# Four wide blocks in place of three, an attention plan that keeps SBUF work out of GpSimd's spans, and query loads into three buffers

## The chip, the cores and the metric

The kernel runs on one core of a Trainium2 chip. The metric is the device time of one execution in microseconds. The core has TensorE (PE; PEld are its weight loads), VectorE (DVE), ScalarE (ACT), GpSimd (POOL) and SyncE (SP), whose queue issues all DMAs here.

## The reference

Two parts, in float32:

```
proj = einsum('bhsd,df->bhsf', x, w_phi)          # x is q or k: 8 x 8 x 576 x 64, f = 128
proj = proj - max(abs(proj), axis=-1)
phi  = concat([exp(proj), exp(-proj)], axis=-1)   # 256 features
kv = einsum('bhsf,bhsd->bhfd', phi(k), v);  z = sum(phi(k), axis=2)
attn = einsum('bhsf,bhfd->bhsd', phi(q), kv) / (einsum('bhsf,bhf->bhs', phi(q), z) + 1e-6)
x = attn, tokens by heads*dims: 4608 x 512
out = gelu(x @ w_in) @ w_out                      # 512 -> 2048 -> 512, gelu with erf
```

## The kernel before, in words

The work is planned as a list of operations on engines (`plan.op`), each with an assumed cost, a rank, the buffers it uses, and for PE a kind. `Plan.order` goes through a schedule: it takes the engine whose next operation can start first, and on it, of those that could start within 0.02 us, the one of lowest rank. An operation can start when what it reads is done and its buffers' slots are free. The result is one fixed order per engine, which the chip runs with semaphores; the assumed costs are not used on the chip. Two things in that planner matter here. For an operation of VectorE that reads no PSUM (`psum=False`) and overlaps a GpSimd operation, it adds a cost `BLOCKED` of 0.9 us once per GpSimd operation. And PE changes between feed-forward work (`kind` "f") and attention work in lumps (`LUMP`, `LINGER`).

**Attention** goes by batch b = 0 to 7, in two halves g of four heads. `k_quad` loads keys (kt) and values (vt), projects them (pk), takes the maximum (mx) and the difference on VectorE, the exponentials (ek) on ScalarE, and sums into kv. `q_pair` handles two heads and half the tokens: a load qt, the projection pq, a copy pc on ScalarE, `partition_all_reduce` with absmax on GpSimd (mb), a difference on VectorE, two exponentials (ef), the numerator pn, and a store to x_d. For b = 0 and 1 (`EB`, `ND`) the denominator comes out of the matmul too; from b = 2 on VectorE forms un and GpSimd sums it over partitions (db). `quotients` loads the denominators (dc), inverts them and stores r_d.

**Weights**: 16 pieces w_i and 16 pieces w_o arrive as 64-bit numbers (raw); `split_weight` turns each into two float32r parts with two steps on ScalarE and five on VectorE. w_o15 is the last.

**Feed-forward**: `block` (narrow, 256 tokens) loads xr and rb, makes xh and xl, and runs 192 matmuls of 256 columns (ph) and 96 of 512 columns (po). `wide_block` (512 tokens) uses seven products in place of eight for the first layer: 336 matmuls of 256 columns (pa, pb) and 192 of 512 (po_po, po_pp), against 384 and 192 in two narrow blocks. It needs combinations of the weights, which `combos` forms on VectorE (tiles sw and sh) and stores in s_d, from where each wide block loads them (s). `JW` is the number of pairs of narrow blocks: with 6 there are 12 narrow and 3 wide blocks. Operations of combos and wide blocks are planned after the last 60 operations of attention (`GATE`). A block's output passes through ob (two slots) to a store.

Of the kernel before, what the change touches and what calls it, by code (L numbers as in the profile page):

```python
# [10 lines left out]
F32 = mybir.dt.float32  # L11
F32R = mybir.dt.float32r
# [15 lines left out]
P = 128  # L28
HS = S // 2
# [30 lines left out]
class Plan:  # L60
# [57 lines left out]
    def order(self, bias):  # L118
        free = dict(self.slots)
        slot_free_at = {t: [0.0] * n for t, n in self.slots.items()}  # L120
        turn = dict.fromkeys(self.slots, 0)
        engines = {}
        for o in self.ops:
            engines.setdefault(o.eng, [])
        clock = dict.fromkeys(engines, 0.0)
        table = [None]
        cand = {e: [] for e in engines}
        for o in self.ops:
            if o.wait == 0:
                cand[o.eng].append(o)  # L130
        done = []
        n = len(self.ops)

        gelus, left_at, dma, dge = [0], [0.0], [0.0], [0.9]

        def start_of(o):
            t = max(clock[o.eng], o.ready)
            if o.table == "exp" and table[0] == "gelu" and gelus[0] % (2 * STICK):
                t = max(t, left_at[0] + PATIENCE)
            seen = {}  # L140
            for b in o.bufs:
                if not b.held and b.tag is not None:
                    f, i = slot_free_at[b.tag], seen.get(b.tag, 0)
                    if len(b.line) <= i or b.line[i] is not b:
                        return None
                    when = f[(turn[b.tag] + i) % len(f)]
                    if when is None:
                        return None
                    t = max(t, when)
                    seen[b.tag] = i + 1  # L150
            return t


        clk = {"i": 0, "full": False, "busy": 0.0}
        last, first = ["f"], {}
        taken = []

        def run(t, work, duty):
            while work > 1e-9:
                i = int(t / self.WINDOW + 1e-9)  # L160
                while clk["i"] < i:
                    use = clk["busy"] / self.WINDOW
                    clk["full"] = use > (0.5 if clk["full"] else self.BUSY)
                    clk["i"] += 1
                    clk["busy"] = 0.0
                speed = 1.0 if clk["full"] else 0.51
                dt = min((i + 1) * self.WINDOW - t, work / speed)
                clk["busy"] += dt * duty
                work -= dt * speed
                t += dt  # L170
            return t

        while len(done) < n:
            best = None
            for e, lst in cand.items():
                if not lst:
                    continue
                opts = []
                for o in lst:
                    t = start_of(o)  # L180
                    if t is not None:
                        opts.append((t, o))
                if not opts:
                    continue
                t0 = min(t for t, _ in opts)
                lim = max(t0, clock[e]) + 0.02
                hold = 0.0
                if e == "pe" and last[0] == "f":
                    t_of = {id(o): max(o.ready, first.setdefault(o.n, t)) for t, o in opts}
                    there = [o for t, o in opts if t <= lim and o.kind != "f"]  # L190
                    if sum(o.cost for o in there) < LUMP and all(lim - t_of[id(o)] < LINGER for o in there):
                        hold = 4000.0
                key = None
                for t, o in opts:
                    if t <= lim:
                        k = o.rank
                        if e == "act" and o.table is not None and o.table != table[0]:
                            k += bias
                        if o.kind != "f":
                            k += hold  # L200
                        if key is None or (k, o.n) < key[0]:
                            key = ((k, o.n), t, o)
                if best is None or key[1] < best[1]:
                    best = key
            if best is None:
                raise RuntimeError("no operation can go")
            _, t, o = best
            cand[o.eng].remove(o)
            cost = o.cost
            if o.eng == "act" and o.table is not None and o.table != table[0]:  # L210
                cost += self.SWITCH
                table[0] = o.table
            if o.eng == "pe":
                if self.SHAPE[last[0]] != self.SHAPE[o.kind]:
                    cost += self.BEHIND[last[0]] + self.BEFORE[o.kind]
                last[0] = o.kind
            if o.eng == "dve" and not o.psum:
                for span in taken[-4:]:
                    if t < span[1] - 0.3 and t + cost > span[0] + 0.3 and not span[2]:
                        span[2] = True  # L220
                        cost += BLOCKED
            if o.eng == "pool":
                taken.append([t, t + cost, False])
            o.start, o.end = t, run(t, cost, o.duty) if o.eng == "pe" else t + cost
            if o.nbytes:
                dge[0] = max(dge[0], t) + 0.55
                dma[0] = max(dma[0], dge[0] + 0.75) + o.nbytes / 350.0
                o.late = dma[0] + 0.15 - o.end
            if o.table == "gelu":
                gelus[0] += 1  # L230
                left_at[0] = o.end
            clock[o.eng] = o.end
            for b in o.bufs:
                if b.tag is not None and not b.held:
                    f = slot_free_at[b.tag]
                    b.slot = turn[b.tag]
                    f[b.slot] = None
                    turn[b.tag] = (b.slot + 1) % len(f)
                    b.held = True
                    assert b.line.pop(0) is b  # L240
                b.left -= 1
                if b.left == 0 and b.tag is not None:
                    slot_free_at[b.tag][b.slot] = o.end + o.late + self.HOP[o.eng]
            for u in o.users:
                u.wait -= 1
                u.ready = max(u.ready, o.end + o.late + (self.HOP if u.eng != o.eng else self.SAME)[o.eng] + (MARGIN if u.eng == "pe" != o.eng and o.end > 130.0 else 0.0))
                if u.wait == 0:
                    cand[u.eng].append(u)
            done.append(o)
        self.done = done  # L250
        return max(o.end + o.late for o in done)
# [37 lines left out]
def fused_kernel(ctx: ExitStack, tc: tile.TileContext, qT, kT, va, w_st, w_in, w_out, out):  # L289
    nc = tc.nc  # L290
# [11 lines left out]
    sb = {t: plan.pool(spool, t, n) for t, n in SLOTS.items()}  # L302
    PS = dict(pp=1, kv=1, pn=1, ph=2, po=1)
    ps = {t: plan.pool(ppool, t, n, False) for t, n in PS.items()}
    op = plan.op
# [167 lines left out]
    def q_pair(b, p, kvs, rank, halves=(0, 1)):  # L473
# [4 lines left out]
        for half in halves:  # L478
            nm = f"{b}_{p}_{half}"
            ss = slice(half * HS, half * HS + HS)  # L480
            qt = sb["qt"]([P, HS] if b < EB else [P, 2, HS], F32, f"qt_{nm}")
            if b < EB:
                op("sp", 0.06, lambda qt=qt, ss=ss: nc.sync.dma_start(out=qt(), in_=qT[b, p, :, ss]), w=[qt], kb=147, **k(1))
            else:
                for i in range(2):
                    op("sp", 0.06, lambda qt=qt, ss=ss, i=i: nc.sync.dma_start(
                        out=qt()[64 * i : 64 * i + 64], in_=qT[b, p, :, ss].rearrange("(j d) t -> d j t", j=2)), w=[qt], kb=147, **k(1))
# [172 lines left out]
    def combos(rank):  # L660
        plan.stream = "c"
        lo, hi = slice(0, 256), slice(256, 512)
        for q in range(4):
            for i in range(2):
                k = dict(rank=rank((2 * q + i) / 8))
                ws = [sb["ob"]([P, 512], F32, f"sw_{q}_{i}_{x}") for x in range(2)]
                hs = [sb[tag]([P, 512], F32R, f"sh_{q}_{i}_{tag}") for tag in ("db", "qt")]
                for x in range(2):
                    c = wi[i + 2 * x, q]
                    tt("dve", dve(512), ws[x], lambda c=c: c()[:, 0].bitcast(F32), lambda c=c: c()[:, 1].bitcast(F32), ALU.add, [c], [ws[x]], also=[*ws, *hs], **k)  # L670
# [17 lines left out]
    def wide_block(j, rank):  # L688
# [55 lines left out]
        for u in range(NU):  # L744
# [3 lines left out]
            sm = {}  # L748
            for s in (2, 3, 1, 4):
                m = sm[s] = sb[RING[s - 1]]([P, 2, 2, P], F32R, f"s{s}_{j}_{u}")  # L750
                op("sp", 0.06, lambda m=m, q=q, e=e, s=s: nc.sync.dma_start(out=m().bitcast(F32), in_=s_d[q]()[SUMS.index(s), e]), r=[s_d[q]], w=[m], kb=262, rank=rk - 20)
            A = ps["ph"]([P, 2, TB], F32, f"pa_{j}_{u}")
            Bk = ps[("kv", "pn")[u % 2]]([P, 2, TB], F32, f"pb_{j}_{u}")
            own = lambda c, f, q=q: (lambda i, w: wi[c + i, q]()[:, w, f % 4 * P : f % 4 * P + P], [wi[c, q], wi[c + 1, q]])
# [98 lines left out]


SB = 2
JW = 6
AHEAD = 1.5
AHEADW = 1.5
MARGIN = 0.8
CR = 100.0  # L860
CSPAN = 100.0
GATE = 60
T15 = 901.4
BIAS = 40
STICK = 2
PATIENCE = 2.5
URGE = -1000.0
EARLY = 37.5
WPACE = 3.996
WSPAN = 24.5  # L870
WARM = 4
EARLY_PK = ("pp", "po")
EARLY_E = ("ek", "xh", "ek", "xl")
BLOCKED = 0.9
HOLD2 = 0.0
EB = 2
KB = 0
EPACE = 20.0
TF = 90.0
ND = 2  # L880
LUMP = 2.5
LINGER = 3.0
PAIR_K = 0.43
PAIR_Q = 0.7
PAIR_N = 1.18
PAIR_V = 0.125
PULL = -2000.0
LEAD = 167.4
HOLD = 44.6
WR = -13.5  # L890
ATR = -21.1
T0 = 57.4
VERBOSE = False


# [36 lines left out]
```

## Time and profile before

| | |
|---|---|
| median of 3 runs | 1150.15 us (1148.31 to 1151.35) |
| the profiled execution | 1147.43 us, of which the span in the profile is 1145.7 us |
| PE busy | 1097.1 us, 96% of the span |
| DVE, ACT, POOL busy | 696.2, 662.2, 321.5 us |
| mean granted clock of TensorE | 0.98 |

The shares are means over stages. Up to about 207 us the weights are converted and attention of the first batches runs; up to about 790 us attention and narrow blocks are interleaved; then there are narrow blocks alone, and from about 875 us the three wide blocks.

### The profile page before, as it was taken

The numbers are of one execution on the slowest core, as the hardware profiler recorded it, in microseconds if no ns is written. First come the engines' busy times: TensorE is split into PE (matmuls) and PEld (weight loads), VectorE is DVE, ScalarE is ACT, GpSimd is POOL, SyncE is SP. The second block draws the span as 40 slices with busy tenths as digits, with TensorE's granted clock in tenths as the row PEclk, the third lists the DMA queues.
The fourth block names the chain that finished last, engine by engine and source line by source line (L and its number), as shares of the span: only waits on it lengthen the run. The fifth ranks groups of instructions, "written<-read, shape, count | busy, mean of one in ns | idle before, by whom it ended". The sixth has DMA issues, their size and how long they took to land.

```text
span 1145.7 us, 22254 instructions
## 1 busy us (share of the span) xinstructions
PE 1097.1 (96%) x8952; PEld 920.4 (80%) x8952; DVE 696.2 (61%) x1153; ACT 662.2 (58%) x1045; POOL 321.5 (28%) x116
## 2 busy tenths in 40 slices
PE   7878987999999999999999999999999999999997
PEld 4545766888887888888888888889889888898986
DVE  6897889665856867656466566554655534534331
ACT  5776857767777787776878778762112222222322
POOL 3323023343644546352445445450000000000000
PEclk9998987999999999999999999999999999999999
DMA  7676631324141332413132231205543624623420
GB/s 248 222 230 215 198 104 33 95 64 129 48 124 43 93 83 86 106 62 102 55 93 80 79 88 49 69 18 125 152 129 115 190 84 115 196 94 114 136 83 37
DMA packets 112439, 125.59 MB, mean 110 GB/s; under 512 B 27648, under 2 KB 87200, under 8 KB 112336
## 3 DMA queue, kind: packets, MB, share of 16 engines
q1 hardware_dynamic: 112336, 124.17, 36.6%
q8 instruction: 70, 1.15, 0.4%
q14 instruction: 33, 0.27, 0.1%
HBM read 96.57 MB, written 27.56 MB: 108 GB/s over the span
## 4 chain that ended last, share of the span: by engine, by line
PE 72%; DVE 9%; DMA 6%; issue 4%; SPq 3%; ACT 3%; POOL 2%; DVEq 0%; ACTq 0%; POOLq 0%
PE po L308 18%; PE ph L308 18%; PE kv L308 6%; PE pb L308 5%; PE po_pp L308 5%; PE pn L308 5%; PE po_po L308 5%; PE pa L308 4%; PE pq L308 3%; PE pk L308 3%; POOL mb L513 1%; SPq L708 1%; DMA qt<-in_qT_dram 1%; DMA rp<-r_d 1%; DVE gl L334 1%
## 5 line engine op out<-in xcount | busy, mean ns | idle before, releaser
L308 PE MATMUL ph<-xh,w_i 128*128 128x256 f32 x1536 | 299.9, 284 | 1.6 <-DVE gl L334 1.2
L308 PEld LDWEIGHTS ph<-xh,w_i 128*128 128x128 f32 x1536 | 248.2, 190 | 9.6 <-issue 2.2
L308 PE MATMUL po<-w_o,gh 128*128 128x512 f32 x768 | 246.4, 402 | 1.9 <-ACT ob L328 1.9
L513 POOL PARTITION_ALL_REDUCE mb<-pc x64 | 147.8, 2311 | 285.6 <-ACT pc L328 247.1
L548 POOL PARTITION_ALL_REDUCE db<-un x48 | 175.3, 3652 | 161.6 <-DVE un L545 123.4
L308 PE MATMUL ph<-xl,w_i 128*128 128x256 f32 x768 | 218.7, 285 | 0.0
L308 PEld LDWEIGHTS po<-w_o,gh 128*128 128x128 f32 x768 | 137.7, 190 | 31.4 <-issue 2.2
L308 PE MATMUL po<-w_o,gl 128*128 128x512 f32 x384 | 152.9, 398 | 0.6 <-DVE gl L334 0.6
L308 PEld LDWEIGHTS ph<-xl,w_i 128*128 128x128 f32 x768 | 146.1, 190 | 3.3
L519 ACT ACTIVATE ef<-pc 128x576 f32<-128x576 f32 x128 | 83.1, 680 | 59.1 <-DVE pc L334 58.8
L334 DVE TENSOR_TENSOR gl<-ph,gh 128x512 fp32r<-128x512 f32 x96 | 65.8, 686 | 84.5 <-ACT ph L636 81.2
L308 PEld LDWEIGHTS kv<-vt,ek 128*64 128x64 f32 (+1 forms) x2560 | 85.6, 140 | 36.7 <-ACT ek L447 14.1
L635 ACT ACTIVATE gh<-ph 128x512 fp32r<-128x512 f32 x96 | 57.5, 599 | 90.5 <-PE ph L308 83.1
L308 PE MATMUL kv<-vt,ek 128*64 128x65 f32 (+1 forms) x2560 | 97.7, 228 | 9.6 <-ACT ek L447 9.3
L308 PE MATMUL pn<-ef,kvn 128*64 128x288 f32 (+1 forms) x512 | 98.1, 425 | 1.2 <-ACT xo L328 1.0
L635 ACT ACT_TABLE_LOAD x76 | 97.5, 1283 | 1.5 <-PE ph L308 0.3
L308 PEld LDWEIGHTS po<-w_o,gl 128*128 128x128 f32 x384 | 73.0, 190 | 18.5 <-DVE gl L334 1.6
L794 ACT ACTIVATE gh<-pa 128x512 fp32r<-128x512 f32 x24 | 14.4, 599 | 123.1 <-PE po_pp L308 86.1
L447 ACT ACTIVATE ek<-ek 128x512 f32<-128x512 f32 (+1 forms) x120 | 70.1, 587 | 24.8 <-DVE ek L334 23.0
L334 DVE TENSOR_TENSOR pc<-pc,mb 128x576 f32<-128x576 f32 x64 | 65.4, 1021 | 29.7 <-POOL mb L513 29.4
L430 DVE TENSOR_REDUCE mx<-pk 128x4 f32<-128x512 f32 (+1 forms) x80 | 50.5, 631 | 50.2 <-PE pk L308 50.0
L308 PEld LDWEIGHTS pn<-ef,kvn 128*64 128x64 f32 (+1 forms) x512 | 39.6, 139 | 32.5 <-issue 7.5
(90 smaller groups left out, 1699.5 us busy)
## 6 DMA issues: line engine op xcount, KB each, us to landing
s<-s_d SPq DMA_DIRECT2D x96, 256.0 KB
qt<-in_qT_dram SPq DMA_DIRECT2D x112, 144.0 KB
vt<-in_va_dram SPq DMA_DIRECT2D x16, 585.0 KB
kt<-in_kT_dram SPq DMA_DIRECT2D x16, 576.0 KB
out_dram<-ob SPq DMA_DIRECT2D x36, 256.0 KB
raw_i<-in_w_in_dram SPq DMA_DIRECT2D x16, 512.0 KB
raw_o<-in_w_out_dram SPq DMA_DIRECT2D x16, 512.0 KB
x_d<-xo SPq DMA_DIRECT2D x48, 144.0 KB
```

The costliest lines, as they stand in the source:

```text
L308: return tc.keep_in_program_order(nc.tensor.matmul(*a, **kw))
L334: op(eng, cost, lambda: e.tensor_tensor(out=dst(), in0=a(), in1=b(), op=o), r=r, w=w, **kw)
L430: op("dve", dve(256 * n, True), lambda xs=xs, mx=mx: nc.vector.tensor_reduce(out=mx()[:, 0].rearrange("p (j i) -> p j i", j=2), in_=xs(), ...
L447: op("act", act(256 * n, b < SB), lambda at=at, es=es, s=s: nc.scalar.activation(es[s](), at(), AF.Exp, scale=1.0 - 2.0 * s), r=[of], w=[e ...
L513: op("pool", 2.2, lambda mb=mb, pc=pc: nc.gpsimd.partition_all_reduce(mb(), pc(), P, bass_isa.ReduceOp.absmax), r=[pc], w=[mb], **k(1))
L519: op("act", act(2 * HS), lambda ef=ef, pc=pc, s=s: nc.scalar.activation(ef()[:, s], pc(), AF.Exp, scale=1.0 - 2.0 * s), r=[pc], w=[ef], ta ...
L548: op("pool", 3.7, lambda db=db, un=un: nc.gpsimd.partition_all_reduce(db(), un(), P, bass_isa.ReduceOp.add), r=[un], w=[db], **k())
L635: op("act", act(2 * TB, True) + 0.016, lambda gh=gh, ph=ph: nc.scalar.activation(gh(), ph(), AF.Gelu), r=[ph], w=[gh], table="gelu", rank= ...
L708: op("sp", 0.06, lambda b=b, i=i, h=h, s=s, n=n, o=o, z=z, to=rp[z]: nc.sync.dma_start(out=to()[64 * i : 64 * i + 64, :, o : o + n], in_=r ...
L794: op("act", act(2 * TB, psum) + 0.016, lambda gh=gh, at=at: nc.scalar.activation(gh(), at(), AF.Gelu), r=[at], w=[gh], table="gelu", rank= ...
```

## The change

`JW` becomes 5: 10 narrow and 4 wide blocks. The planner no longer adds a cost for VectorE operations without PSUM in a GpSimd operation; it moves their start to the end of a span that begins with the GpSimd operation and lasts 1.4 us for the maximum (`LOCK_MAX`) and 2.4 us for the sum (`LOCK_SUM`). Operations that read PSUM may start inside. In the batches 0 and 1 the query loads use three tags (qt, gh, gl) in turn. `combos` takes its tiles from ek, mb and pc in place of ob, db and qt, and a wide block's loads of s are planned after all stores to s_d. Ranks and paces are new numbers.

```diff
+            if o.eng == "dve" and not o.psum and taken and taken[-1][0] <= t < taken[-1][1]:
+                t = taken[-1][1]
             return t
...
-            if o.eng == "dve" and not o.psum:
-                for span in taken[-4:]:
-                    if t < span[1] - 0.3 and t + cost > span[0] + 0.3 and not span[2]:
-                        span[2] = True
-                        cost += BLOCKED
             if o.eng == "pool":
-                taken.append([t, t + cost, False])
+                taken.append((t, t + (LOCK_MAX if cost < 3.0 else LOCK_SUM)))
...
-            qt = sb["qt"]([P, HS] if b < EB else [P, 2, HS], F32, f"qt_{nm}")
+            qt = sb[("qt", "gh", "gl")[(2 * p + half) % 3] if b < EB else "qt"]([P, HS] if b < EB else [P, 2, HS], F32, f"qt_{nm}")
...
-                ws = [sb["ob"]([P, 512], F32, f"sw_{q}_{i}_{x}") for x in range(2)]
-                hs = [sb[tag]([P, 512], F32R, f"sh_{q}_{i}_{tag}") for tag in ("db", "qt")]
+                tags = ("ek", "ek") if i == 0 else ("mb", "pc")
+                ws = [sb[tag]([P, 512], F32, f"sw_{q}_{i}_{x}") for x, tag in enumerate(tags)]
+                hs = [sb[tag]([P, 512], F32R, f"sh_{q}_{i}_{x}") for x, tag in enumerate(tags)]
...
-JW = 6
+JW = 5
-T15 = 901.4
+T15 = 947.637
-EARLY = 37.5
-WPACE = 3.996
-WSPAN = 24.5
+EARLY = -18.706
+WPACE = 2.424
+WSPAN = 0.0
-BLOCKED = 0.9
+LOCK_MAX = 1.4
+LOCK_SUM = 2.4
-TF = 90.0
+TF = 76.044
-LUMP = 2.5
-LINGER = 3.0
+LUMP = 1.066
+LINGER = 2.713
-LEAD = 167.4
+LEAD = 320.754
```

SP's queue at the program's start, before (qt, kt, vt are query, key and value loads, raw are weights; the first two numbers are batch and pair or half):

```order
L321 DMA wst_68<-in_w_st_dram 128x128
L483 DMA qt_0_0_0_70<-in_qT_dram 128x288
L399 DMA kt_0_0_72<-in_kT_dram 128x1152
L401 DMA vt_0_0_74<-in_va_dram 128x1170
L399 DMA kt_0_1_76<-in_kT_dram 128x1152
L401 DMA vt_0_1_78<-in_va_dram 128x1170
L349 DMA raw_i0_0_80<-in_w_in_dram 128x512
L349 DMA raw_i1_0_89<-in_w_in_dram 128x512
L349 DMA raw_i2_0_97<-in_w_in_dram 128x512
L483 DMA qt_0_0_1_106<-in_qT_dram 128x288
```

and after the change:

```order
L318 DMA wst_68<-in_w_st_dram 128x128
L396 DMA kt_0_0_70<-in_kT_dram 128x1152
L398 DMA vt_0_0_72<-in_va_dram 128x1170
L396 DMA kt_0_1_74<-in_kT_dram 128x1152
L398 DMA vt_0_1_76<-in_va_dram 128x1170
L480 DMA qt_0_0_0_78<-in_qT_dram 128x288
L480 DMA qt_0_0_1_80<-in_qT_dram 128x288
L480 DMA qt_0_1_0_82<-in_qT_dram 128x288
L480 DMA qt_0_2_0_85<-in_qT_dram 128x288
L346 DMA raw_i0_0_87<-in_w_in_dram 128x512
```

The first query load moved behind the keys and values, and three more query loads moved ahead of the first weight.

VectorE's queue around the last weight piece, before. The first of these rows is the 275th operation of this queue:

```order
L353 TENSOR_SCALAR wt_o15_2245<-wt_o15_2245 128x512
L545 SCALAR_TENSOR_TENSOR un_2_1_0_2231<-ef_2_1_0_2145,kvn_2_0_1_1893,un_2_1_0_2231 128x288
L355 TENSOR_SCALAR wt_o15_2245<-wt_o15_2245 128x512
L545 SCALAR_TENSOR_TENSOR un_2_1_0_2231<-ef_2_1_0_2145,kvn_2_0_1_1893,un_2_1_0_2231 128x288
L357 SCALAR_TENSOR_TENSOR wt_o15_2245<-raw_o15_1625,wt_o15_2245 128x512
L334 TENSOR_TENSOR gl_1_0_2278<-ph_1_0_2160,gh_1_0_2257 128x512
L359 SCALAR_TENSOR_TENSOR wt_o15_2245<-raw_o15_1625,wt_o15_2245 128x512
L334 TENSOR_TENSOR pc_2_1_1_2235<-pc_2_1_1_2235,mb_2_1_1_2247 128x576
L430 TENSOR_REDUCE mx_2_1_2_2312<-pk_2_1_2_2261 128x2
L334 TENSOR_TENSOR w_o15_2309<-wt_o15_2245,w_o15_2309 128x512
```

and after, where the first row is the 276th:

```order
L352 TENSOR_SCALAR wt_o15_2246<-wt_o15_2246 128x512
L331 TENSOR_TENSOR w_o14_2277<-wt_o14_2199,w_o14_2277 128x512
L354 SCALAR_TENSOR_TENSOR wt_o15_2246<-raw_o15_1093,wt_o15_2246 128x512
L539 TENSOR_SCALAR un_2_1_0_2279<-ef_2_1_0_2261,kvn_2_0_1_1767 128x288
L356 SCALAR_TENSOR_TENSOR wt_o15_2246<-raw_o15_1093,wt_o15_2246 128x512
L542 SCALAR_TENSOR_TENSOR un_2_1_0_2279<-ef_2_1_0_2261,kvn_2_0_1_1767,un_2_1_0_2279 128x288
L427 TENSOR_REDUCE mx_2_1_4_2317<-pk_2_1_4_2201 128x4
L331 TENSOR_TENSOR gl_1_0_2321<-ph_1_0_2214,gh_1_0_2288 128x512
L331 TENSOR_TENSOR w_o15_2319<-wt_o15_2246,w_o15_2319 128x512
```

In both orders w_o15 is the 284th operation of VectorE, beside the same unit of the feed-forward (gl of block 1, unit 0); the key maxima beside it (mx of batch 2) are two units further on.

VectorE's queue where the weight combinations begin, before (numbers after sw and sh: quarter, step, piece; gl is feed-forward work):

```order
L334 TENSOR_TENSOR sw_0_0_1_8667<-sw_0_0_1_8667,sw_0_0_0_8658 128x256
L330 CAST sh_0_0_db_8694<-sw_0_0_0_8658 128x512
L330 CAST sh_0_0_qt_8696<-sw_0_0_1_8667 128x512
L334 TENSOR_TENSOR gl_9_6_8707<-ph_9_6_8643,gh_9_6_8690 128x512
L334 TENSOR_TENSOR sw_0_0_0_8658<-sw_0_0_0_8658,sh_0_0_db_8694 128x512
```

and after:

```order
L331 TENSOR_TENSOR sw_0_0_1_8148<-w_i2_0_381 128x512
L331 TENSOR_TENSOR gl_8_2_8167<-ph_8_2_8094,gh_8_2_8129 128x512
L331 TENSOR_TENSOR sw_0_0_1_8148<-sw_0_0_1_8148,sw_0_0_0_8134 128x256
L331 TENSOR_TENSOR sw_0_1_0_8186<-w_i1_0_331 128x512
L331 TENSOR_TENSOR sw_0_0_0_8134<-sw_0_0_0_8134 128x256
```

They began beside block 9, unit 6, and now begin beside block 8, unit 2; two steps now overlap.

## Rows read from the trace of the kernel before

**Rows 1.** The page: busy time by engine, and PE in 40 slices.
```profile
PE 1097.1 (96%) x8952; PEld 920.4 (80%) x8952; DVE 696.2 (61%) x1153; ACT 662.2 (58%) x1045; POOL 321.5 (28%) x116
...
PE   7878987999999999999999999999999999999997
```

**Rows 2.** Windows: stretch, length, busy by engine (instructions), clock, DMA share, GB/s.
```profile
0.00:112.00 112.00, 89.25 (x967) 55.06 (x968) 90.40 (x149) 76.40 (x168) 32.16 (x19) 0.91 0.72 230
112.00:207.00 95.00, 82.68 (x643) 68.39 (x642) 85.21 (x136) 67.14 (x104) 26.64 (x9) 0.89 0.40 112
207.00:790.00 583.00, 581.75 (x5206) 489.44 (x5205) 360.88 (x551) 427.67 (x606) 262.68 (x89) 1.00 0.28 79
790.00:875.00 85.00, 82.43 (x515) 73.82 (x514) 51.13 (x100) 17.47 (x32) 0.00 (x0) 0.98 0.47 133
875.00:1146.00 271.00, 261.00 (x1628) 233.73 (x1626) 108.59 (x220) 73.51 (x136) 0.00 (x0) 1.00 0.38 117
```

**Rows 3.** Waits of PE, 0 to 207 us: total us, times, longest.
```profile
PE pq L308 <- DVE ek L334: 10.4, 3, 4.8
PE pq L308 <- DMA qt<-in_qT_dram: 10.1, 6, 3.8
PE kv L308 <- ACT ek L447: 9.3, 7, 2.3
```

**Rows 4.** Groups by form of DVE, 10 to 207 us: busy us, mean ns.
```profile
L430 DVE TENSOR_REDUCE mx<-pk 128x4 f32<-128x512 f32 x22 | 15.0, 681 | 6.6 <-PE pk L308 6.6
...
L359 DVE SCALAR_TENSOR_TENSOR wt_i<-raw_i,wt_i 128x512 uint32<-128x512 uint32 x16 | 12.8, 812 | 0.1
...
L334 DVE TENSOR_TENSOR pk<-pk,mx 128x512 f32<-128x512 f32 x16 | 11.0, 690 | 0.1
...
L357 DVE SCALAR_TENSOR_TENSOR wt_i<-raw_i,wt_i 128x512 uint32<-128x512 uint32 x16 | 10.7, 684 | 0.2
L353 DVE TENSOR_SCALAR wt_i<-wt_i 128x512 f32<-128x512 f32 x16 | 10.4, 665 | 0.0
...
L330 DVE CAST qh<-qt 128x576 fp32r<-128x576 f32 x4 | 4.9, 1232 | 0.8 <-DMA qt<-in_qT_dram 0.8
...
L334 DVE TENSOR_TENSOR xr<-xr,rb 128x1024 f32<-128x1024 f32 x3 | 3.7, 1225 | 7.9 <-DMA rb<-r_d 3.8 <-DMA kt<-in_kT_dram 3.0 <-DMA x_d<-xo 1.1
```

**Rows 5.** Timeline, 110 to 116 us, DVE and POOL: start, us, and what.
```profile
111.08 0.75 DVE L353 TENSOR_SCALAR wt_i<-wt_i 128x512 f32<-128x512 f32 x2
...
111.41 2.59 POOL L513 PARTITION_ALL_REDUCE mb<-pc  x1 [5.95 <-ACT pc L328]
...
111.75 2.54 DVE L355 TENSOR_SCALAR wt_i<-wt_i 128x512 uint32<-128x512 uint32 x2
```

**Rows 6.** Groups of POOL, 0 to 207 us: busy us, mean ns.
```profile
L513 POOL PARTITION_ALL_REDUCE mb<-pc x20 | 47.1, 2359 | 135.7 <-ACT pc L328 112.3 <-DVE wt_i L357 18.3 <-DVE un L542 3.2
```

**Rows 7.** Waits of PE, 790 to 1146 us.
```profile
PE po_pp L308 <- ACT ob L328: 2.4, 1, 2.4
PE po L308 <- ACT ob L328: 1.9, 1, 1.9
PE pa L308 <- DVE u L334: 1.5, 1, 1.5
```

**Rows 8.** The chain that ended last, 845 to 864 us: start, us, what.
```profile
843.41 1.91 DMA s_d<-sw
...
846.06 7.38 PE po L308 x24
...
857.62 2.86 PE ph L308 x24
860.48 2.77 PE po L308 x12
```

**Rows 9.** The chain that ended last, whole span: a run of key matmuls.
```profile
582.42 1.70 PE kv L308 x48
```

**Rows 10.** Windows: the stretch of block 3, columns as in rows 2.
```profile
329.00:399.00 70.00, 69.29 (x663) 58.36 (x663) 46.59 (x67) 51.84 (x74) 36.40 (x12) 1.00 0.36 97
```

More of the change, by code (lines that the diff above doesn't have):

```diff
@@ L750, in wide_block @@
                 m = sm[s] = sb[RING[s - 1]]([P, 2, 2, P], F32R, f"s{s}_{j}_{u}")
-                op("sp", 0.06, lambda m=m, q=q, e=e, s=s: nc.sync.dma_start(out=m().bitcast(F32), in_=s_d[q]()[SUMS.index(s), e]), r=[s_d[q]], w=[m], kb=262, rank=rk - 20)
+                op("sp", 0.06, lambda m=m, q=q, e=e, s=s: nc.sync.dma_start(out=m().bitcast(F32), in_=s_d[q]()[SUMS.index(s), e]), r=s_d, w=[m], kb=262, rank=rk - 20)
             A = ps["ph"]([P, 2, TB], F32, f"pa_{j}_{u}")
@@ L862 @@
 GATE = 60
-T15 = 901.4
+T15 = 947.637
 BIAS = 40
 STICK = 2
-PATIENCE = 2.5
+PATIENCE = 2.457
 URGE = -1000.0
-EARLY = 37.5
-WPACE = 3.996
-WSPAN = 24.5
+EARLY = -18.706
+WPACE = 2.424
+WSPAN = 0.0
 WARM = 4
@@ L887 @@
 PULL = -2000.0
-LEAD = 167.4
+LEAD = 320.754
 HOLD = 44.6
-WR = -13.5
-ATR = -21.1
-T0 = 57.4
+WR = -15.951
+ATR = -24.818
+T0 = 50.594
 VERBOSE = False
```

## The prediction

> **What bounds the kernel now.** I read the page first: PE is busy for 96% of the span, and its slices show that the rest lies almost wholly in the first seven of forty [rows 1]. The reader should see that two different kernels run one after the other. Windows by stage show it [rows 2]. From 207 to 790 us PE is busy 581.75 of 583 us at full clock, with VectorE at 62% and ScalarE at 73%: here only less PE work shortens the time. Up to 207 us it is another matter: PE is busy 171.9 of 207 us at a mean clock of 0.91 and then 0.89, while VectorE is busy 175.6 us, and 85.2 of the last 95. The waits of PE there name operations of VectorE and ScalarE and query loads [rows 3], and behind the first two stands VectorE, which converts the weights. From 790 us on PE is nearly full again.
>
> So the span is the time at which VectorE finishes the last weight piece w_o15, about 207 us, and the PE work that is then left.
>
> How VectorE loses time is seen in its groups up to 207 us [rows 4]. Two forms of equal size and kind can be set side by side: L357 on w_i takes 684 ns and L359 on w_i 812 ns, though both read two tensors of 512 columns; the short L353 takes 665 ns in the mean, although two of them ran in 0.75 us undisturbed [rows 5]. The timeline shows the cause: a GpSimd reduction began at 111.41 us and took 2.59 us, and the two VectorE operations beside it took 2.54 us in place of 0.75 [rows 5]. The excess over the undisturbed length, added over all forms of that view, is some 24 us (L353 on w_i: 16 x 0.25 = 4; L359 on w_i: 16 x 0.13 = 2; qh: 4 x 0.8 = 3; the other weight forms carry most of the rest). There are 20 reductions of the maximum [rows 6] and 3 sums in it, so about 1 us for each. Forms that read PSUM are not stretched: mx at 681 and pk at 690 ns [rows 4]. About 20 us more of VectorE's time after 10 us is idle, of which 7.9 us wait for what xr needs.
>
> **The change part by part.**
>
> *A fourth wide block.* It takes 336 short matmuls in place of 384, and as many long ones. 24 short ones take 2.86 us [rows 8], so 48 x 0.119 = 5.7 us go. The seams between wide blocks cost 1.5 and 2.4 us (a wait for VectorE's u, one for ob) [rows 7], and one seam more is there: +2.0, bounds 1.5 to 2.4.
>
> *The combinations.* They now lie beside blocks 8 and 9 in place of 9 to 11. Their tiles leave ob, where the output of block 10 had to wait for a store to s_d; PE waited 1.9 us for that [rows 7], and the 24 long matmuls behind it took 7.38 us instead of twice 2.77 [rows 8]. That is 3.7 us; I take 3 off, with bounds 0 and 3.7, since the cover is shorter now. The cover: after the last attention matmul come all but a little of two narrow blocks, 2 x (192 x 0.119 + 96 x 0.231) = 90 us, and in the whole stretch of 85 us before wide block 6 VectorE was busy 51 us, combinations and all [rows 2]. If the cover were gone, VectorE's work and a store and load beyond it would stand on PE's path.
>
> *Tables.* Two narrow blocks fewer have some 30 fewer changes of ScalarE's table. ScalarE has 27% left in the middle stage [rows 2]; worth nothing.
>
> *VectorE's order in the first stage.* In the order w_o15 is operation 284 of VectorE before and after. Ahead of PE's first matmul that reads it are 36 short feed-forward matmuls fewer (4.3 us) and 96 of kv (0.035 us each, 3.4 us [rows 9]) and 16 of pk more, so the PE work left after it is the same but for the terms above. What counts is when w_o15 is done. Nothing that the order shows takes work off VectorE; what can go are the 24 us of stretching and some of the idle time. PSUM work fit to fill the GpSimd spans is there (mx 15.0 us and pk 11.0 us among 175 [rows 4]), but it comes when PE gives it. I take 7 us off, 30% of the stretching: nearer to no gain than to all of it, since operations were already planned with 0.9 us for each reduction, and an in-order queue that drifts by a microsecond against the plan misses the spans. Bounds: 24 off, or 10 on.
>
> The bound on the other side is for the loads. All 32 weight pieces are now issued before the first rb; before it were 24. That makes about 28 MB in place of 23. The first 112 us moved 230 GB/s at a share of 0.72 [rows 2], so 28 MB need about 88 us at a full share: it fits, but each load queues behind more. If query loads make PE wait twice as long as the 10.1 us of now [rows 3], 10 us come on. On the other hand three buffers in place of one let queries come before they are wanted. This may take those 10.1 us away; as VectorE bounds this stage I count nothing for it.
>
> *Denser attention.* The order puts 224, 226 and 220 attention matmuls beside blocks 4 to 6; the densest before was 198 beside block 3. In block 3's stretch VectorE was busy 46.6 and ScalarE 51.8 of 70 us, and PE lost 0.7 us [rows 10]. Scaled by 226/198 that is 53 and 59 us, in about 72: 74% and 82%. I take +2 for the three blocks; bounds 0 and 18 (below).
>
> The sum: -5.7 + 2.0 - 3 - 7 + 2 = -11.7 us. The profiled execution took 1147.4, so 1135.7; the median of the runs stands 2.7 above that execution, so 1138 us.
>
> **The rivals.** *The plan hits the spans* (0.17): all 24 us of stretching go in the first stage, and the other terms stand: -5.7 + 2 - 3 - 24 + 2 = -28.7, 1121 us. For it: every stretched form is one without PSUM. Against it: PSUM work is a quarter of what VectorE does there.
>
> *The spans are missed* (0.20): w_o15 comes as late as now, -4.7 us, 1145 us. For it: the two operations beside the 2.59 us reduction were held almost to its end [rows 5], and the planned span of 1.4 us ends long before; an operation put at its end would still be held for another 1.0 us of the mean 2.36 [rows 6], as long as the present stretch. Against it: the mean stretch of 1 us says that most reductions let VectorE go on sooner. The Trainium skill (SBUF — State Buffer, Who interferes with whom) has the port held for the whole instruction and the other engine fully blocked; by that rule this rival is right, and the pair in rows 5 agrees, the mean does not.
>
> *Dense attention makes PE wait* (0.16), the slower side. From 112 to 207 us, with VectorE busy 90% of the time, PE was idle 12.3 of 95 us, 13% [rows 2]. If VectorE or ScalarE gets there in two of the three dense blocks, 13% of 140 us, 18 us, come on in place of 2: 1154 us. It decides when the three blocks lose over 14 us, 6% of their 216 us. Against it: 74% and 82% are estimates below that level, and 73% of ScalarE cost PE nothing.
>
> **How the numbers follow.** A measurement tells 0.3%, 3.5 us, from no change: 1146.7 to 1153.6. My forecast has 0.47, with a range of its own of 1130 to 1147. The cases together hold eight in ten from 1119 to 1153. Faster: 0.47 + 0.17 + half of the missed spans, 0.10, is 0.74. Same: the other 0.10 and a little of the last case, 0.12. Slower: 0.14.
>
> **What would show it.** PE should become full near 200 us, when w_o15 is done, and the stretched forms L353 and L355 should have shorter means. If w_o15 comes at 207 with the old means, the second rival is right. In the densest blocks PE should be idle under 1 us in 70; waits of pk, pn or ph for VectorE or ScalarE of several microseconds there would bring the slower case. No wait of po for ob should stand before the first wide block, and three seams of about 2 us after it. A wait of the first wide block for s or for b would show that the cover of the combinations was too short.

## The result, and the profile after

The changed kernel takes 1130.15 us in the median of 4 runs (1129.26 to 1131.98), against 1149.59 us for the kernel before beside it; the ratio is 0.983, with a 95% interval of 0.981 to 0.985. The profiled executions lie closer together, 1131.98 against 1147.43 us, a difference of 15.5 us, and this difference is what the traces can account for.

The page of the changed kernel, busy time by engine and PE with its granted clock in 40 slices, answers to [rows 1]:

```profile
PE 1080.8 (96%) x8904; PEld 908.4 (80%) x8904; DVE 717.5 (63%) x1209; ACT 626.9 (55%) x1023; POOL 321.0 (28%) x116
...
PE   7898999999998999999999999999999999899997
...
PEclk9999999999999999999999999999999999999999
```

The 48 matmuls are gone (8904 against 8952). The hole in the first slices is narrower, and the granted clock there is higher, as the windows below show: 0.98 in both early stages, against 0.91 and 0.89 before [rows 2]. But single slices later, which read 9 before, now read 8. Its windows, in stages that end with the last weight piece and with attention, show both (columns as in [rows 2]):

```profile
0.00:112.00 112.00, 93.58 (x1107) 58.06 (x1108) 95.29 (x158) 83.17 (x184) 36.29 (x20) 0.98 0.83 277
112.00:184.00 72.00, 68.55 (x594) 58.01 (x593) 70.77 (x129) 60.22 (x91) 15.37 (x5) 0.98 0.27 75
184.00:689.00 505.00, 489.37 (x4533) 407.14 (x4532) 345.18 (x508) 367.21 (x533) 265.58 (x90) 1.00 0.28 81
689.00:1131.00 442.00, 429.31 (x2676) 385.17 (x2675) 206.21 (x416) 116.32 (x216) 3.79 (x2) 0.99 0.43 128
```

In the second of these VectorE is busy 70.8 of 72 us: it has become full. The loads of the first stage ran at a share of 0.83 and 277 GB/s in place of 0.72 and 230. In the third PE is idle 15.6 of 505 us; in the whole stretch from 207 to 790 us before it was 1.25 of 583 [rows 2]. When the last weight piece was done is read from the timeline of VectorE (start, us, what):

```profile
182.22 0.68 DVE L331 TENSOR_TENSOR gl<-ph,gh 128x512 fp32r<-128x512 f32 x1
182.81 0.68 DVE L331 TENSOR_TENSOR w_o<-wt_o,w_o 128x512 fp32r<-128x512 f32 x1
```

It ended at 183.5 us; before, at 207.3. PE's waits up to 184 us (total us, times, longest) answer to [rows 3]:

```profile
PE pn L305 <- ACT xo L325: 7.5, 9, 2.1
PE kv L305 <- ACT ek L444: 5.9, 8, 1.3
...
PE pq L305 <- DMA qt<-in_qT_dram: 0.4, 1, 0.4
```

The wait for query loads fell from 10.1 to 0.4 us, and that of pq for ek from 10.4 to nothing. VectorE's groups from 10 to 184 us answer to [rows 4]:

```profile
L427 DVE TENSOR_REDUCE mx<-pk 128x4 f32<-128x512 f32 x24 | 16.4, 682 | 6.8 <-PE pk L305 6.8
...
L356 DVE SCALAR_TENSOR_TENSOR wt_i<-raw_i,wt_i 128x512 uint32<-128x512 uint32 x16 | 12.2, 767 | 0.1
...
L350 DVE TENSOR_SCALAR wt_i<-wt_i 128x512 f32<-128x512 f32 x16 | 9.4, 592 | 0.2
...
L331 DVE TENSOR_TENSOR xr<-xr,rb 128x1024 f32<-128x1024 f32 x3 | 4.2, 1400 | 1.1 <-DMA d_d<-xo 1.1
...
L327 DVE CAST qh<-qt 128x576 fp32r<-128x576 f32 x4 | 1.9, 466 | 0.0
```

The short L350 (L353 before) went from 665 to 592 ns, L356 (L359) from 812 to 767, the cast to qh from 1232 to 466; what xr waits for fell from 7.9 to 1.1 us.

PE's waits from 184 to 689 us, where the kernel before had 1.1 us of such waits in all, show what was lost again:

```profile
PE pq L305 <- DVE ek L331: 7.6, 10, 1.2
PE pk L305 <- DVE ek L331: 4.2, 4, 2.0
PE pq L305 <- DVE qh L331: 2.8, 2, 2.2
PE pn L305 <- ACT xo L325: 1.0, 2, 0.6
```

pk and pq of these batches share one PSUM buffer, which VectorE's ek frees; PE's in-order queue stands still with feed-forward work behind. VectorE's single records ahead of these sixteen waits for VectorE, 14.6 us together, divide them. Ahead of twelve, 10.5 us, an operation shortly before in its queue had been held beside a GpSimd reduction, though in four of them for less time than PE waited. Ahead of four, 4.1 us, none had: there VectorE had itself stood idle, for ScalarE, for loads or for a sum of GpSimd.

**An account in four terms.** The matmuls of a trace stand in the same sequence as in the program's order, so each can be named. At their steady spacing (0.118 us for 256 columns, 0.230 for 512, 0.034 for kv, 0.081 for pk, 0.14 for pn, 0.13 to 0.15 for pq; 3.5 us for the eight matmuls on idle data at the program's start) the work of all is 1034.3 us before and 1028.6 after. The rest of the time is a loss of three parts: up to the end of w_o15, from there to the last attention matmul, and after that.

| us | w_o15 done | work by then | early loss | middle loss | late loss | last matmul |
|---|---|---|---|---|---|---|
| before | 207.3 | 130.1 | 77.2 | 17.2 | 10.9 | 1139.5 |
| changed | 183.5 | 131.1 | 52.4 | 32.2 | 10.8 | 1124.0 |
| e1 old rule | 200.1 | 129.0 | 71.1 | 35.8 | 9.4 | 1144.9 |
| e2 one query buffer | 198.0 | 128.0 | 70.0 | 25.0 | 10.4 | 1134.1 |
| e3 old pace | 228.3 | 149.7 | 78.6 | 29.0 | 8.6 | 1144.9 |
| e4 six pairs | 181.9 | 131.1 | 50.8 | 33.8 | 5.6 | 1124.5 |
| e5 larger lumps | 190.0 | 134.8 | 55.2 | 22.0 | 52.0 | 1157.9 |
| e6 larger lumps, six pairs | 189.7 | 133.9 | 55.8 | 21.8 | 5.4 | 1117.3 |
| e7 no sums | 182.6 | 131.1 | 51.5 | 16.9 | 9.3 | 1106.3 |
| e8 before with three parts | 188.7 | 130.5 | 58.2 | 18.5 | 7.2 | 1118.2 |
| e9 before with the rule | 199.0 | 129.8 | 69.2 | 15.8 | 6.9 | 1126.1 |
| e10 before with the pace | 194.9 | 127.2 | 67.7 | 18.8 | 11.3 | 1132.1 |
| e11 before with rule and pace | 185.3 | 127.6 | 57.7 | 21.8 | 11.3 | 1125.1 |
| e12 as e6, longer spans | 198.8 | 133.0 | 65.8 | 19.3 | 4.4 | 1123.8 |

Each row is one profiled execution, and executions of one kernel lie up to 10 us apart (e11, 1124.83 to 1135.15), so small differences between rows are not to be read. A loss is not all idle time: of the middle loss of 17.2 before, PE was idle for only about 1 us, and of the 32.2 after for 15.6 us; the rest, about 16 us in both, is matmuls that came slower than their steady spacing, and what slowed them stays open. From before to after: 24.8 us less early, 5.7 us less work, 15.0 us more in the middle, 0.1 less late; together the 15.5 us.

Two more measures are used below. VectorE's *stretched time* is what its operations beside a GpSimd operation took beyond the usual length of the same form with none beside it; counts of it can differ by 1 to 2 us. Its *idle time* is the length of a window less VectorE's busy time in it.

### The profile page after: what moved, and what is told of

The parts are those of the page before. It is cut to its first block, busy times and chain, and to the rows that moved or that the text cites. A ratio compares the mean times of both kernels' runs of the same rounds, so it can differ in the third digit from the quotient of the medians.

```text
span 1130.2 us, 22251 instructions
## 1 busy us (share of the span) xinstructions
PE 1080.8 (96%) x8904; PEld 908.4 (80%) x8904; DVE 717.5 (63%) x1209; ACT 626.9 (55%) x1023; POOL 321.0 (28%) x116
## 4 chain that ended last, share of the span: by engine, by line
PE 60%; DVE 19%; ACT 7%; DMA 6%; issue 3%; SPq 3%; POOL 2%; DVEq 0%; POOLq 0%; ACTq 0%
PE ph L305 13%; PE po L305 12%; PE po_pp L305 7%; PE pb L305 7%; PE po_po L305 7%; PE pa L305 5%; PE kv L305 3%; PE pn L305 2%; DVE pc L331 2%; DVE mx L427 2%; DVE qh L331 2%; PE pq L305 2%; POOL db L545 2%; PE pk L305 2%; DVE qh L327 1%
## 5 line engine op out<-in xcount | busy, mean ns | idle before, releaser
L305 PE MATMUL ph<-xh,w_i 128*128 128x256 f32 x1280 | 250.6, 284 | 0.0
L305 PEld LDWEIGHTS ph<-xh,w_i 128*128 128x128 f32 x1280 | 206.8, 190 | 6.6 <-issue 1.3
L305 PE MATMUL po<-w_o,gh 128*128 128x512 f32 x640 | 204.4, 401 | 0.0
L305 PE MATMUL ph<-xl,w_i 128*128 128x256 f32 x640 | 182.2, 285 | 0.0
L305 PEld LDWEIGHTS po<-w_o,gh 128*128 128x128 f32 x640 | 113.2, 188 | 26.2 <-issue 3.9
L305 PE MATMUL po<-w_o,gl 128*128 128x512 f32 x320 | 125.8, 393 | 0.0
L305 PEld LDWEIGHTS ph<-xl,w_i 128*128 128x128 f32 x640 | 121.6, 190 | 2.3
L792 ACT ACTIVATE gh<-pa 128x512 fp32r<-128x512 f32 x32 | 19.1, 598 | 160.0 <-PE po_pp L305 111.6
L305 PE MATMUL po_pp<-w_o,gh 128*128 128x512 f32 x256 | 80.7, 397 | 4.4 <-ACT ob L325 4.4
L305 PE MATMUL po_po<-w_o,gh 128*128 128x512 f32 x256 | 79.8, 393 | 0.0
L305 PE MATMUL pb<-b,s 128*128 128x256 f32 x576 | 79.2, 282 | 0.0
```

Of the source, the lines that this page charges most:

```text
L305: return tc.keep_in_program_order(nc.tensor.matmul(*a, **kw))
L792: op("act", act(2 * TB, psum) + 0.016, lambda gh=gh, at=at: nc.scalar.activation(gh(), at(), AF.Gelu), r=[at], w=[gh], table="gelu", rank= ...
```

## The experiments

Two questions stood: which part gave the early 25 us, and what took 15 us back. Theory 1 on the first was that the ranks and paces did it. Theory 2, on the second, was that the denser attention makes PE wait for VectorE.

**e1, the rule of before in the changed kernel.**

```diff
-            if o.eng == "dve" and not o.psum and taken and taken[-1][0] <= t < taken[-1][1]:
-                t = taken[-1][1]
...
+            if o.eng == "dve" and not o.psum:
...
+                        cost += BLOCKED
...
```

> The changed kernel with the planner's rule of before (a cost of 0.9 us, no moved start); all else as changed. In the changed kernel the last weight piece w_o15 was done at 183.5 us, 24 us earlier than before. Theory 1 (the early 24 us come mainly from the ranks and paces that bring the weights in sooner, so that VectorE has no idle time): w_o15 near 188, time 1132 to 1138. Rival (the 24 us come from the moved starts): w_o15 past 200, time 1146 or more.

Measured: 1153.99 us, ratio to before 1.004 (1.002 to 1.007); w_o15 at 200.1. Both numbers of the rival came; the early loss grew by 18.7 us, so theory 1 in this form falls. VectorE's stretched time up to w_o15 was 22.6 us, against 14.5 in the changed kernel and 23.7 before; its idle time from 10 us on was 15.1 us, against 9.3 and 23.1.

**e2, one query buffer.**

```diff
-            qt = sb[("qt", "gh", "gl")[(2 * p + half) % 3] if b < EB else "qt"]([P, HS] if b < EB else [P, 2, HS], F32, f"qt_{nm}")
+            qt = sb["qt"]([P, HS] if b < EB else [P, 2, HS], F32, f"qt_{nm}")
```

> The changed kernel with one buffer for the query loads of batches 0 and 1. Theory 1: w_o15 within 5 us of 183.5, time 1130 to 1136. Rival (the early gain comes from the query loads, whose waits fell from 10.1 to 0.4 us on PE): w_o15 at 193 or later, time 1140 or more.

Measured: 1140.75 us, 0.994 (0.992 to 0.996). PE's wait for query loads came back, 8.0 us in 7 times, and the early loss grew by 17.6 us; the middle loss shrank by 7. Both numbers of the rival came (w_o15 at 198.0). VectorE's idle time from 10 us to w_o15 was 21.5 us, against 9.3 in the changed kernel.

**e3, the old early numbers.**

```diff
-EARLY = -18.706
-WPACE = 2.424
-WSPAN = 0.0
-TF = 76.044
-WR = -15.951
+EARLY = 37.5
+WPACE = 3.996
+WSPAN = 24.5
+TF = 90.0
+WR = -13.5
```

> The changed kernel with the numbers EARLY, WPACE, WSPAN, TF and WR of before, which set when weights and first queries are loaded and converted and when the first block may start. Theory 1: w_o15 near 205 and the time 1143 to 1153, as most of the early gain is lost. Rivals (rule or buffers): w_o15 within 6 us of 183.5 and the time under 1138.

Measured: 1152.58 us, 1.004 (1.001 to 1.006). As theory 1 expected in time; w_o15 came later still, at 228.3, but with 18.6 us more PE work done by then, so that the early loss, 78.6, is that of before. Any one of three parts taken out gave most of the early gain back. That asked for the other direction, e8 to e11.

**e4, six pairs of narrow blocks** (`JW = 6`), all else as changed.

> The changed kernel with six pairs of narrow blocks, so three wide blocks. Theory 1 (a fourth wide block is worth 5.7 us of matmuls less one seam of 1 to 3 us): 1133 to 1136, w_o15 as in the changed kernel, and the 14 us that the middle stage loses stay. Rival (the fourth wide block, by leaving two narrow blocks fewer beside attention, is what makes the middle stage lose): the middle stage loses under 5 us and the time is 1122 to 1127.

Measured: 1131.93 us, 0.986 (0.983 to 0.989), a microsecond under the expected range. The order up to the end of attention is that of the changed kernel, and the middle loss stayed (33.8), so the rival falls. The fourth wide block is worth 5.7 us of work, and gives 5.2 of them back in the late loss, 10.8 against 5.6. Other rows say the same: 8.6 to 10.4 with four wide blocks (e1, e2, e3, e7), 5.4 and 4.4 with three and the new tiles of the combinations (e6, e12). The late waits of PE in the changed kernel show where:

```profile
PE po_pp L305 <- ACT ob L325: 4.4, 2, 3.0
PE pa L305 <- DVE u L331: 1.4, 1, 1.4
```

With three wide blocks it was one wait of po_pp for ob, of 2.3 us, and one of pa. The chain at the dearer seam of the changed kernel says why it is long (start, us, what): the store that frees ob is issued behind loads of the next wide block in SP's queue.

```profile
954.03 2.76 DMA rp<-r_d
...
959.28 0.47 SPq L706
...
959.80 0.60 SPq L706
...
960.50 6.12 DMA out_dram<-ob
...
966.64 0.59 ACT ob L325
```

Right behind this wait of 3.0 us the granted clock of TensorE was at its lower level, 1.2 GHz, for 3.4 us (a window, columns as in [rows 2]); in e4 it stays at the upper level there.

```profile
967.50:970.90 3.40, 3.40 (x9) 2.63 (x9) 3.03 (x6) 1.08 (x2) 0.00 (x0) 0.50 0.74 264
```

**e5, larger lumps.**

```diff
-LUMP = 1.066
-LINGER = 2.713
+LUMP = 2.5
+LINGER = 3.0
```

> The changed kernel with LUMP 2.5 and LINGER 3.0 as before: PE takes attention in larger lumps, so that attention beside blocks 3 to 6 falls from 198, 224, 226, 220 matmuls to 172, 190, 184, 186 and runs on beside block 8. From the end of w_o15 to the last attention matmul the kernel before lost 17 us against the work of its matmuls, the changed kernel 32. Theory 2 (density makes PE wait for VectorE there): this loss falls to 17 to 23, but attention ends one block later, so the first wide block has half the cover for the weight combinations, and 5 to 15 us come on there: 1120 to 1132. Rival (the loss goes with the moved starts, which keep VectorE waiting in the plan): the loss stays over 28, time 1133 or more.

Measured: 1164.42 us, 1.012 (1.010 to 1.015). The middle loss fell to 22.0, as theory 2 said, but the late loss rose to 52.0, far past the 5 to 15 us. One wait of PE from 727 us on made it:

```profile
PE pa L305 <- DMA s<-s_d: 40.6, 1, 40.6
```

Attention now ended beside block 8, so one narrow block was left to cover the combinations, and the first load of s stood behind all stores to s_d.

**e6, larger lumps and six pairs.**

> As the one before, with six pairs of narrow blocks and three wide blocks, so the cover of the combinations is whole again. Theory 2: the loss of the middle stage falls to 17 to 23 and that at the end stays near 6: 1115 to 1122, faster than the changed kernel. Rival: as with six pairs alone, 1132.

Measured: 1125.29 us, 0.979 (0.977 to 0.981): faster than the changed kernel, whose interval begins at 0.981. The middle loss was 21.8, the late one 5.4; the early one grew by 3.4, which the expectation had left out, and so the time lies 3 us over its range. Between e4 and e6 only the lumps differ, and the middle loss falls from 33.8 to 21.8 us, PE's waits for ek in this stage from 12.8 to 3.3. The table agrees: with the smaller lumps and the sums it is 25.0 to 35.8 us, with the larger lumps 15.8 to 22.0.

**e7, without the sums on GpSimd.**

```diff
-            op("pool", 3.7, lambda db=db, un=un: nc.gpsimd.partition_all_reduce(db(), un(), P, bass_isa.ReduceOp.add), r=[un], w=[db], **k())
+            op("pool", 3.7, lambda db=db: nc.gpsimd.memset(db()[:1], 1.0), r=[un], w=[db], **k())
```

> The changed kernel in the same order on every engine, with the 48 sums over partitions on GpSimd left out (a short memset of one row stands in their place, so the denominators of batches 2 to 7 are not formed). Theory 2, in the form that VectorE is late because GpSimd holds the port: the stretched time of VectorE in the middle stage falls from 75 to under 35 us, the loss of that stage from 32 to 17 to 24, time 1117 to 1124. Rival (VectorE and ScalarE are late by the density of their own work): the stretched time falls as much, but the loss stays over 27 and the time over 1126.

Measured: 1114.33 us, 0.969 (0.967 to 0.971), 3 us under the expected range. Its window of the middle stage stands against the third window of the changed kernel above, with the same instructions but for the sums:

```profile
183.00:672.00 489.00, 485.22 (x4531) 405.74 (x4531) 297.26 (x511) 366.31 (x533) 121.25 (x89) 1.00 0.30 83
```

VectorE is busy 297 in place of 345 us for 511 and 508 instructions; its stretched time there fell from 75.1 to 24.6 us, and the middle loss from 32.2 to 16.9, what it was before the change. ScalarE's work is the same (366 and 367 us). So the rival falls: the work that is left on VectorE and ScalarE does not make the loss by itself. The holding alone does not make it either. In the kernel before, VectorE was stretched by some 66 us in this stage and the loss was 17.2; e6 keeps the sums, and 63.4 us of stretching, and lost 21.8. What the changed kernel lost takes both, dense attention and VectorE held beside GpSimd. One thing is not divided here: without the sums VectorE's waits for the buffer that a sum reads went too (11.5 us in the changed kernel), while its waits for the maxima rose from 10.4 to 19.1 us.

**e8, the kernel before with three parts of the change**: the rule, the three buffers and the five numbers of e3.

> The kernel before with three early parts of the change: moved starts, three query buffers, and EARLY, WPACE, WSPAN, TF and WR as changed; six pairs, and its other numbers. Each of the three taken out of the changed kernel cost 18 to 26 us of the 24. If they work only together, as these runs suggest: w_o15 less the PE work done by then falls from 77 to 50 to 58 us, time 1122 to 1132. Rival (the runs without one part were slow because the other numbers are tuned for it, not for the part's sake): over 68 us, time over 1138.

Measured: 1126.26 us, 0.980 (0.977 to 0.983), early loss 58.2; the time is in its range and the loss at the edge of its own. The whole change took 1130.15: the part of it with four wide blocks and dense attention brings nothing over this.

**e9, the rule alone; e10, the five numbers alone; e11, both**, each in the kernel before.

> The kernel before with the moved starts alone. All three early parts together took w_o15 less the PE work done by then from 77 to 58 us and the time to 1126. If the parts work only together: 68 to 77 us here, time 1137 to 1149. Rival (the moved starts are the part that counts): under 62 us, time under 1132.

> The kernel before with EARLY, WPACE, WSPAN, TF and WR as changed, alone. If the parts work only together: 68 to 80 us, time 1137 to 1152. Rival (the weights' earlier loads are the part that counts): under 62 us, time under 1132.

> The kernel before with the moved starts and the five numbers, without the three query buffers. If the third part is needed, as the changed kernel without it suggests (70 us): 64 to 75 us, time 1134 to 1146. Rival: under 60 us and the time as with all three, 1124 to 1130.

Measured: e9 1135.13 us, 0.988 (0.983 to 0.992); e10 1143.23 us, 0.994 (0.990 to 0.997); e11 1132.91 us, 0.983 (0.978 to 0.988). The early loss fell by 8.0 us with the rule, by 9.5 with the numbers and by 19.5 with both. That the parts work only together falls: they about add up. No expectation came whole: e9 was 2 us faster than its range, with a loss inside it; e10's loss lay just under its range; e11 had the rival's loss but not its time. With the rule alone VectorE's stretched time up to w_o15 fell from 23.7 to 15.2 us, by 8.5, about as much as the early loss; the time fell by more, 15.8 us, as the middle and late losses were smaller too. But less stretching is not the rule's mark alone: in e10, which moves no starts, it fell by some 7 us as well. Idle time from 10 us to w_o15 was still 21.1, 20.3 and 19.4 us in the three, against 23.1 before. The three buffers added nothing to the early loss on this side (57.7 without, 58.2 with them), against 17.6 us in e2: in e8 the idle time was 13.4, 6 us less than in e11, and the stretching some 5 us more. Why one buffer costs so much in the changed kernel's other numbers stays open: the planner's order shifts as a whole with each edit, and a single undone part is compared with numbers set for it.

**e12, longer spans**, in the kernel of e6: the planner takes a maximum to hold VectorE for 2.2 us, and a sum for 3.6.

```diff
-LOCK_MAX = 1.4
-LOCK_SUM = 2.4
+LOCK_MAX = 2.2
+LOCK_SUM = 3.6
```

> As with larger lumps and six pairs (1125 us, early loss 56, middle loss 22, VectorE stretched 15 us up to w_o15 and 63 us in the middle stage), with LOCK_MAX 2.2 and LOCK_SUM 3.6 in place of 1.4 and 2.4, near the whole length of the reductions. If the second hold, after the planned spans, makes much of the stretching that is left: 63 falls under 45 us and the time to 1117 to 1124. Rival (the stretching that is left comes from the chip's drift against the plan, and longer spans only keep VectorE idle): it stays over 52 us, time 1125 to 1140.

Measured: 1133.29 us, 0.985 (0.983 to 0.988), 8 us slower than e6. VectorE's stretched time in the middle stage fell from 63.4 to 38.6 us, and up to w_o15 from 15.1 to 10.0, as the first theory said; but the middle loss fell only from 21.8 to 19.3, and the early loss grew from 55.8 to 65.8. The time is the rival's, and so is its idle VectorE: from 10 us to w_o15 VectorE stood idle for 26.8 us in place of 12.0. In the stage that waits for VectorE's queue, 5.1 us of held time were exchanged for 14.8 of idle time. In the windows of e12 the stage in which the last weight pieces are made is as full as in e6 (74.62 of 78 us there), but it ends 9 us later:

```profile
112.00:200.00 88.00, 75.75 (x667) 63.50 (x666) 84.29 (x150) 62.99 (x99) 13.99 (x5) 0.96 0.25 68
```

What was kept back shows in the first 112 us, where VectorE is busy 80.7 us in 137 instructions, against 94.9 in 158 in e6.

## Why the prediction was right, and which terms were mis-sized

Direction and range held; 1138 was 8 us too high. Two terms were off by 17 and 13 us in opposite directions, and that they nearly cancelled was luck: by the profiled executions the change took 15.5 us, against a sum of 11.7. The other 4.5 us of the 8 lie in no term: the sum was set on a profiled execution 2.7 us under its median, and that of the changed kernel stands 1.8 over its own.

- *What bounds the kernel.* Right: the time is that of the last weight piece and the PE work left after it. The work done by then was indeed the same, 130.1 and 131.1 us.
- *VectorE's order in the first stage*, "I take 7 us off", was the first mis-sized term. It measured 23.8 us at w_o15 (24.8 of early loss), at the bound of 24. The bound was thought of as all of the stretching; what came was of two kinds. The windows from 10 us to w_o15, before and after (columns as in [rows 2]), hold 282 operations of VectorE each:

```profile
10.00:207.30 197.30, 164.75 (x1583) 120.14 (x1584) 174.25 (x282) 141.65 (x268) 58.29 (x23) 0.90 0.56 170
10.00:183.50 173.50, 153.90 (x1672) 112.08 (x1671) 164.22 (x282) 141.81 (x273) 51.48 (x21) 0.98 0.60 193
```

Stretching fell by 9.2 us (23.7 to 14.5), near the 7 taken. The other kind, "some of the idle time", was counted at nothing, although the trace had 20 us of it: it fell by 13.8 us, from 23.1 to 9.3, and 6.8 of that is what xr waited for. That w_o15 is operation 284 in both orders says that VectorE has the same work ahead of it, but not how often the queue runs dry. The three buffers, too, were counted at nothing, "as VectorE bounds this stage"; yet of the kernels run, only those with three buffers and the new numbers have less than 19 us of idle time (9 to 15, but 26.8 with the longer spans of e12). The new numbers with one buffer leave 19 to 22 us (e2, e10, e11), three buffers with the old numbers 25.9 (e3). How the rule, the numbers and the buffers share the 24.8 us is not settled beyond the 19.5 that the first two give together (e11).
- *The loads*, 10 us on: did not come. More was moved sooner, at 277 GB/s, and PE waited 0.4 us for queries.
- *A fourth wide block*: 5.7 us of work went, as counted. The seam is dearer than 2 us: with e4 as the other side the late loss is 5.2 us larger, a wait and the lower clock behind it, so the net is about 0.5 us in the last matmuls (1124.0 and 1124.5) and 1.8 us in the medians, and neither is clear of noise (0.981 to 0.985 and 0.983 to 0.989).
- *The combinations*, 3 off: in e4, with three wide blocks as before, the late loss fell by 5.3 us; no wait of po for ob stands before the first wide block. The wait is there in all five kernels with the old tiles (before, e8 to e11), whose late losses are 6.9 to 11.3, and in none of e4, e6 and e12, with 4.4 to 5.6. So the sign is shown; the size is somewhere from 1 to 7 us. Of the 7.38 us of slow matmuls that the prediction added to the wait, 3.4 us ran at the lower clock:

```profile
846.40:849.80 3.40, 3.40 (x10) 2.63 (x9) 2.24 (x5) 0.00 (x0) 0.00 (x0) 0.50 0.22 83
```

That the cover became shorter, which the text named, decided e5.
- *Denser attention*, +2, was the second mis-sized term: the middle stage lost 15 us more. Blocks 4 to 6 alone, after and before, show most of it:

```profile
390.00:620.00 230.00, 219.49 (x2119) 181.33 (x2118) 161.10 (x239) 168.65 (x247) 123.34 (x42) 1.00 0.30 85
399.00:595.00 196.00, 195.49 (x1753) 165.09 (x1752) 119.86 (x185) 146.30 (x206) 83.48 (x29) 1.00 0.28 80
```

PE was idle for 10.5 us, against 0.5. The rival of the slower side had the right place and a wrong condition: it asked for VectorE or ScalarE to reach 90%. VectorE was busy 70% of this stretch, ScalarE 73%, no more than the prediction's 74% and 82%, and PE waited all the same. What decides is not the share but the delay of one operation, ek, that frees the one PSUM buffer. In most of the waits GpSimd had held an operation ahead of it in VectorE's queue; without the sums the loss was gone (e7), and with larger lumps most of it (e6). Its price, 18 us in place of 2, was near the 15 of the whole stage.
- *The spans are missed*, the second rival, fell. Of the two SBUF operations beside one reduction in [rows 5], the single records show that the first took 1.52 us and ended 1.85 us after the reduction began; only the second, which began after that, was held almost to the reduction's end. That was a second hold, as the last section shows; the planned spans fit most reductions, and the rule alone took 15.8 us off the time (e9). The rule of the whole instruction (the Trainium skill, SBUF — State Buffer, Who interferes with whom) does not agree with this trace: after a maximum of 2.14 us an operation went on 1.17 us after its start, as worked out in the last section. Whether one such record covers several instructions of GpSimd, each with a hold of its own, no trace shows.
- *Tables*: 30 loads of 1.283 us fewer (122 for 152), and ScalarE busy 35 us less. The reason given does not hold: e4, with six pairs, has the same 122, and e6 138, so they go with the order of the plan and not with the number of narrow blocks. No run shows what they are worth in time.

## What to carry to other kernels

Where a stage hands over to another at one operation, count both what is ahead of it in its engine's queue and how much of that queue's time was idle or held: the second part was the larger surprise here. An engine with spare time on average can still stop another one, when one of its operations frees a buffer of which there is one; look at who frees it and at what stands ahead of that operation. A change of several parts with numbers fitted to them should be taken apart from both sides: undone singly every part looked necessary, while two of them added to the kernel before gave 19.5 of the 24.8 us. The part that the title names first, the fourth wide block, was worth next to nothing (e4), and two numbers of the plan, which make the lumps of attention smaller, lost 12 us in the middle stage (e4 against e6).

## What the runs showed of the hardware that was not expected

GpSimd holds VectorE's operations without PSUM in pieces. The timeline of the changed kernel shows a maximum with an operation on SBUF beside it (start, us, what):

```profile
18.66 2.14 POOL L510 PARTITION_ALL_REDUCE mb<-pc  x1 [3.57 <-ACT pc L325]
18.75 1.75 DVE L356 SCALAR_TENSOR_TENSOR wt_i<-raw_i,wt_i 128x512 uint32<-128x512 uint32 x1
```

The operation takes 0.68 us undisturbed and ended at 20.50, so, if it ran at that speed once it was let go, it ran from 19.82 on, 1.17 us after the reduction began and 0.97 before it ended. A sum, with two PSUM operations first:

```profile
168.59 3.97 POOL L545 PARTITION_ALL_REDUCE db<-un  x1 [9.21 <-DVE un L542]
169.02 0.68 DVE L427 TENSOR_REDUCE mx<-pk 128x4 f32<-128x512 f32 x1
169.74 0.69 DVE L331 TENSOR_TENSOR ek<-pk,mx 128x512 f32<-128x512 f32 x1
170.35 1.69 DVE L356 SCALAR_TENSOR_TENSOR wt_o<-raw_o,wt_o 128x512 uint32<-128x512 uint32 x1
```

Both PSUM operations ran at full speed, and the next, reckoned in the same way, went on 2.8 us after the start of the sum, 1.2 before its end. In none of the 14 traces did a VectorE operation that reads PSUM take over 13 ns more beside a reduction than the median of its form alone; operations without PSUM took up to 2.3 us more in the changed kernel. Over the stretched operations of the whole trace the median release is 1.26 us after the start of a maximum and 2.47 after that of a sum, with a smaller group near 1.9 to 2.3 and 3.5 us or more: a second hold, into which operations placed at 1.4 and 2.4 us can still run. e12 bears it out: with planned spans of 2.2 and 3.6 us the stretching in the middle stage fell by 24.8 us. The kernel was 8 us slower all the same: in this plan, whose other numbers were not fitted to the longer spans, planning for the whole hold is dearer than running into its end, where VectorE's queue is what the stage waits for.
